# Chunked attention into a squared-ReLU FFN: V of odd heads in shifted tiles, all loads from SyncE, two groups transposed on TensorE

## The chip, the cores and the metric

The kernel runs on one core of a Trainium2 chip. A core has five engines with instruction streams of their own: TensorE (PE, matrix multiplication; PEld is its weight load), VectorE (DVE), ScalarE (ACT), GpSimd (POOL) and SyncE (SP), which only issues DMA transfers and waits. Each engine works through its own stream in program order and waits on semaphores. SP, ACT and POOL can issue DMAs; 16 DMA engines move the data. The metric is the device time of one execution in microseconds (us); lower is better. Where a profile is quoted, times count from the first instruction, and "span" is the time from the first to the last instruction.

## The reference

```python
# q, k, v: (8, 8, 576, 64) float32; chunk = 64
scores = scale * np.matmul(q_c, k_c.transpose(0, 1, 2, 4, 3))   # 64 x 64 per chunk and head
scores = scores - np.max(scores, axis=-1, keepdims=True)
attn = np.exp(scores)
attn = attn / (np.sum(attn, axis=-1, keepdims=True) + 1e-09)
out = np.matmul(attn, v_c)
x = out.transpose(0, 2, 1, 3).reshape(4608, 512)
h = np.maximum(x @ w_in, 0.0)          # w_in 512 x 2048
return (h * h @ w_out)                 # w_out 2048 x 512, result 4608 x 512 float32
```

Attention is block-diagonal: each chunk of 64 tokens attends to itself alone. Everything is float32 in memory.

## The kernel before, in words

The 4608 tokens form 18 groups of 256 (two tiles of 128, t = 0 and 1). Groups form nine blocks: block 0 is groups 0 to 2, blocks 1 to 7 are two groups each (3 and 4, 5 and 6, and so on), block 8 is group 17. A batch has 576 tokens, so some tiles cross from one batch to the next; `segments` and `runs` split such a load in two.

**Loads.** `qk_pieces(g)` loads q and k of a group with tokens on partitions, one DMA for each of q and k and each run of tokens: 256 KB for a whole tile, in pieces of 256 bytes (one head of one token). `v_pieces(g)` loads V into one of five `v_tiles` that have an extra column of ones per head, so that the values' matmul also gives the softmax's sum. Even heads go to the partition of their token (L100, 128 KB for a whole tile). For odd heads the two halves of a tile change places, so that the matmuls of an even and an odd head can work on different quarters of the array; each half is a DMA of its own (L104, 64 partitions, 64 KB). In the start-up and for groups 2 to 4 SP issues all of them; later the odd-head loads are issued by ACT. `load_w_in` and `load_w_out` load the weights in eight pieces each through five staging buffers; POOL casts each to bf16.

**Attention of a group** has four steps. (1) q and k are brought to head-dimension-on-partitions form in `qkT`. Groups 0 and 1 do it on PE through two FFN banks of PSUM (`transpose_qk_early`), group 2 on PE through an attention bank (`transpose_qk`, T), all others by a cast on POOL (`cast_qk`, C) and a DMA transpose that SP issues (`transpose_qk_dma`, TD, L202). (2) `scores` (SC, L216): 32 matmuls and one exponential on ACT. (3) `values` (AV, L235): matmuls with V, then reciprocal and multiplication on DVE, giving x. (4) x is transposed into `xT`: groups 0 and 1 on PE with copies by ACT (`transpose_x_early`), group 2 on PE with a copy by DVE, all others by DMA transposes from SP (`transpose_x`, XT, L258, two per group).

**FFN of a block.** `ffn_in` runs 16 column tiles of w_in; each is four matmuls (L288), a relu on ACT (L294) and a square on DVE (L295) into `gT`. `ffn_out` runs 16 matmuls per 128 tokens (L304), a copy by ACT (L311) and an output DMA issued by SP (L313).

**Order.** It is written out by hand. After the start-up (loads of groups 0 and 1, attention of both with idle PE time filled by `keep_busy`, then all weight loads and those of groups 2, 3 and 4), a block is a sequence of slots: one slot is four matmuls of the FFN. Block 0 has 56 slots (0 to 15 `ffn_in` for 512 tokens, 16 to 31 for the other 256, 32 to 55 `ffn_out`), a block of two groups has 32 (16 and 16). In each slot from `first_load` on, one more load of the block after next ("far") is issued, and then the attention steps that `plan` puts at this slot, for the next block ("nxt") or for far. Since every engine is in order, a step's place in the slots is its place in the streams of PE, SP, ACT, DVE and POOL alike.

Of the kernel before, what the change touches and what calls it, by code (L numbers as in the profile page):

```python
# [9 lines left out]
FP32 = mybir.dt.float32  # L10
BF16 = mybir.dt.bfloat16
# [5 lines left out]
def kernel(  # L17
# [9 lines left out]
    nc = tc.nc  # L27

    B, H, S, D = q.shape
    n_tokens = B * S  # L30
# [3 lines left out]
    n_hp = H // 2  # L34
# [9 lines left out]
    w_pool = ctx.enter_context(tc.tile_pool(name="w", bufs=1))  # L44
# [16 lines left out]


    NV = 5
    v_tiles = [w_pool.tile([128, 2, H, D + 1], FP32, name=f"v_sb{i}") for i in range(NV)]
    for vt in v_tiles:
        nc.gpsimd.memset(vt[:, :, :, D:D + 1], 1.0)

    def segments(g0, n):
        while n:
            b, s = divmod(g0, S)  # L70
            m = min(n, S - s)
            yield b, s, m
            g0 += m
            n -= m
# [3 lines left out]
    def runs(g):  # L78

        for t in range(GT // 128):  # L80
            p = 0
            for b, s, m in segments(g * GT + t * 128, 128):
                yield t, p, m, b, s
                p += m
# [8 lines left out]
                    out=dst[p:p + m, t, :, :],  # L93
                    in_=src[b, :, s:s + m, :].rearrange("h s d -> s h d"))

    def v_pieces(g, eng=(nc.sync, nc.sync)):

        vt = v_tiles[g % NV]
        for t, p, m, b, s in runs(g):
            yield lambda t=t, p=p, m=m, b=b, s=s: eng[0].dma_start(  # L100
                out=vt[p:p + m, t, 0::2, 0:D],
                in_=v[b, 0::2, s:s + m, :].rearrange("h s d -> s h d"))
            for c in range(0, m, 64):
                yield lambda t=t, p=64 - (p + c), b=b, s=s + c: eng[1].dma_start(  # L104
                    out=vt[p:p + 64, t, 1::2, 0:D],
                    in_=v[b, 1::2, s:s + 64, :].rearrange("h s d -> s h d"))

    def go(pieces):
        for f in pieces:
            f()  # L110

    def load_w_in(i, eng=nc.sync):
        cols = slice(i * 256, (i + 1) * 256)
        st = wst_pool.tile([128, 1024], FP32, name="w_st").rearrange("p (a f) -> p a f", a=n_dt)
        eng.dma_start(
            out=st, in_=moe_w_in[:, cols].rearrange("(a p) f -> p a f", p=128))
        nc.gpsimd.tensor_copy(out=w_in_bf[:, :, cols], in_=st)  # L117
# [37 lines left out]
    def transpose_qk_early(g, k_copy):  # L155
        qkT = att_pool.tile([128, 2, 2, n_hp, 128], BF16, name="qkT", bufs=4)
        state["qkT", g] = qkT
        banks = [ps_ffn.tile([128, 512], FP32, name="ps_ffn").bitcast(BF16) for _ in range(2)]
        for t in range(2):
            for which in range(2):  # L160
                srcb = qk[g][which].bitcast(BF16)
                for hp in range(n_hp):
                    c0 = t * 512 + hp * 128
                    nc.tensor.transpose(  # L164
                        out=banks[which][:, c0:c0 + 128],
                        in_=srcb[:, t, 2 * hp:2 * hp + 2, 1::2],
                        identity=ident)
        for which, copy in enumerate((nc.vector.tensor_copy, k_copy)):
            copy(out=qkT[:, which].rearrange("c t h q -> c (t h q)"), in_=banks[which])  # L169

    def transpose_x_early(g, t):
        j, c = place[g]
        if j not in xTs:
            xTs[j] = att_pool.tile([128, n_dt, BT], BF16, name="xT", bufs=2)
        psb = ps_ffn.tile([128, 512], FP32, name="ps_ffn").bitcast(BF16)
        x = state.pop(("x", g, t))
        for hp in range(n_hp):
            nc.tensor.transpose(  # L178
                out=psb[:, hp * 128:(hp + 1) * 128],
                in_=x[:, hp].rearrange("p a d -> p (a d)"),  # L180
                identity=ident)
        nc.scalar.copy(  # L182
            out=xTs[j][:, :, c + t * 128:c + (t + 1) * 128],
            in_=psb[:, 0:512].rearrange("p (h t) -> p h t", h=n_hp))

    def keep_busy(n):
        ps = ps_ffn.tile([128, 512], FP32, name="ps_ffn")
        for _ in range(n):
            nc.tensor.matmul(out=ps[:, 0:128], lhsT=ident, rhs=ident, start=True, stop=True)  # L189
# [35 lines left out]

    def values(g):
        e = state.pop(("e", g))
        vb = v_tiles[g % NV].bitcast(BF16)
        for t in range(2):
            ps = ps_att.tile([128, 2, 512], FP32, name="ps_att")  # L230
            for hp in range(n_hp):
                for a in range(2):
                    for p in range(2):
                        c = p ^ a
                        nc.tensor.matmul(  # L235
                            out=ps[64 * p:64 * p + 64, a, hp * (D + 1):(hp + 1) * (D + 1)],
                            lhsT=e[64 * c:64 * c + 64, a, hp, t, :],
                            rhs=vb[64 * c:64 * c + 64, t, 2 * hp + a, 1::2],
                            start=True, stop=True)
            o = ps[:, :, 0:n_hp * (D + 1)].rearrange("p a (h d) -> p a h d", d=D + 1)  # L240
            rec = att_pool.tile([128, 2, n_hp], FP32, name="rec", bufs=4)
            nc.vector.reciprocal(out=rec, in_=o[:, :, :, D])  # L242
            x = att_pool.tile([128, n_hp, 2, D], BF16, name="x", bufs=6)
            state["x", g, t] = x
            nc.vector.tensor_tensor(  # L245
                out=x.rearrange("p h a d -> p a h d"),
                in0=o[:, :, :, 0:D],
                in1=rec.to_broadcast([128, 2, n_hp, D]),
                op=ALU.mult)
# [25 lines left out]

    T, C, TD = transpose_qk, cast_qk, transpose_qk_dma
    SC, AV, XT = scores, values, transpose_x

    gTs = {}

    def ffn_in(j, c, n):
# [32 lines left out]
                if ft % 4 == 3:  # L314
                    yield

    def pieces(grps, eng=(nc.sync, nc.sync)):
        for g in grps:
            yield from qk_pieces(g)
        for g in grps:  # L320
            yield from v_pieces(g, eng)

    go(qk_pieces(0))
    go(qk_pieces(1))
    go(v_pieces(0))
    go(v_pieces(1))
    transpose_qk_early(0, nc.scalar.copy)
    keep_busy(8)
    SC(0)
    load_w_in(0, nc.scalar)  # L330
    keep_busy(8)
    transpose_qk_early(1, nc.vector.tensor_copy)
    keep_busy(8)
    SC(1)
    keep_busy(8)
    AV(0)
    keep_busy(6)
    AV(1)
    transpose_x_early(0, 0)
    transpose_x_early(0, 1)  # L340
    keep_busy(10)
    transpose_x_early(1, 0)
    transpose_x_early(1, 1)

    for i in range(1, 4):
        load_w_in(i)
    go(pieces([2]))
    for i in range(4, 8):
        load_w_in(i)
    for i in range(8):  # L350
        load_w_out(i)
    go(pieces(blocks[1]))

    for j, grps in enumerate(blocks):
        nxt = blocks[j + 1] if j + 1 < len(blocks) else []
        far = blocks[j + 2] if j + 2 < len(blocks) else []
        loads = pieces(far, (nc.sync, nc.scalar))
        plan = {}

        def at(slot, f, g):  # L360
            plan.setdefault(slot, []).append((f, g))

        if j == 0:
            first_load = 30
            for slot, f in ((7, T), (7, SC), (8, AV), (10, XT)):
                at(slot, f, 2)
            for i, g in enumerate(nxt):
                for slot, f in ((26, C), (30, TD), (43, SC), (46, AV), (47, XT)):
                    at(slot if f is SC else slot + 3 * i, f, g)
            for i, g in enumerate(far):  # L370
                at(46 + 2 * i, C, g)
                at(50 + 3 * i, TD, g)
            phases = [ffn_in(0, 0, 512), ffn_in(0, 512, 256), ffn_out(0)]
        else:
            first_load = 0
            for i, g in enumerate(nxt):
                for slot, f in ((1, SC), (5, AV), (8, XT)):
                    at(slot if f is SC else slot + 3 * i, f, g)
            for i, g in enumerate(far):
                at(14 + 2 * i, C, g)  # L380
                at(19 + 3 * i, TD, g)
            phases = [ffn_in(j, 0, len(grps) * GT), ffn_out(j)]
        slot = 0
        for phase in phases:
            for _ in phase:
                if slot >= first_load:
                    for f in loads:
                        f()
                        break
                for f, g in plan.get(slot, []):  # L390
                    f(g)
                slot += 1
        go(loads)
# [30 lines left out]
```

## Time and profile before

| | |
|---|---|
| median of 3 executions | 332.95 us (332.71 to 335.0) |
| the profiled execution's own time | 334.0 us |
| its span | 332.2 us |
| mean granted TensorE clock | 0.941 |
| PE busy | 289.4 us (87%) |
| ACT, DVE, POOL busy | 129.5, 110.1, 51.1 us |
| DMA | 58.35 MB in 172797 packets, 162016 of them under 512 B |
| chain that ended last | PE 70%, SP's queue 13%, DMA 10% |

The page gives busy time per engine, then the span in 40 slices with the busy share in tenths, the clock granted to PE and the DMA engines' share; then the chain of work that ended last, the costliest groups of instructions, and the DMA issues with the time to landing. A group's row ends with the idle time of its engine just before it and the work that ended this idle time. In a timeline the bracket at the end of a row says the same of a single stretch. A row with SPq or ACTq is an instruction of the queue of SyncE or ScalarE, mostly the issue of a DMA. DMA shares can exceed 1 where packets overlap.

### The profile page before, as it was taken

The page shows a single profiled execution, that of the slowest core. Times are in us where ns is not written, and L with a number is a line of the kernel's source. Part 1 is how long each engine was busy: PE and PEld are TensorE (multiplying, and loading weights), DVE is VectorE, ACT ScalarE, POOL GpSimd, SP SyncE. Part 2 cuts the span into 40 slices and gives each one's busy share as a digit, 9 for nine tenths or more (in the row PEclk, how much of TensorE's full clock was granted, in tenths as well). Part 3 has the DMA queues.
Part 4 walks back from the last instruction along what each step waited for, and adds up shares of the span by engine and source line. Part 5 has one row for each costly group of instructions (what it writes and reads, how often), then busy time and mean ns, then how long its engine had stood idle before and what let it go on. Part 6 is the DMA issues. An engine that isn't in the chain of part 4 may idle for free.

```text
span 332.2 us, 6218 instructions
## 1 busy us (share of the span) xinstructions
PE 289.4 (87%) x2488; PEld 142.4 (43%) x2488; DVE 110.1 (33%) x237; ACT 129.5 (39%) x221; POOL 51.1 (15%) x58
## 2 busy tenths in 40 slices
PE   2769699901964899999999999999999999999995
PEld 1653356401331444444444444444444444444572
DVE  0132398000221281067029206801820570162050
ACT  1324565101112452374265227415632751562261
POOL 1121276402200130022004101300220110000000
PEclk9956999975697799999999999999999999999999
DMA  9999899969968999799969999998999985110101
GB/s 172 227 235 158 271 386 270 193 134 214 231 139 183 213 180 172 179 214 171 201 175 193 197 213 206 194 201 205 164 172 218 236 90 126 65 32 33 65 33 63
DMA packets 172797, 58.35 MB, mean 176 GB/s; under 512 B 162016, under 2 KB 166112, under 8 KB 172768
## 3 DMA queue, kind: packets, MB, share of 16 engines
q1 hardware_dynamic: 158096, 54.02, 77.4%
q10 hardware_dynamic: 14672, 3.94, 8.1%
q8 instruction: 19, 0.31, 0.4%
q14 instruction: 10, 0.08, 0.1%
HBM read 36.70 MB, written 9.44 MB: 139 GB/s over the span
## 4 chain that ended last, share of the span: by engine, by line
PE 70%; SPq 13%; DMA 10%; DVE 3%; issue 1%; ACT 1%; ACTq 0%; POOL 0%
PE ps_ffn L304 34%; PE ps_ffn L288 32%; DMA v_sb<-in_v_dram 6%; SPq L92 5%; DMA qkT<-qkb 3%; SPq L104 3%; DVE gT L295 2%; SPq L100 2%; PE ps_att L235 2%; PE ps_att L216 1%; DMA w_st<-in_moe_w_in_dram 1%; SPq L258 1%; SPq L202 1%; ACT rl L294 1%; DVE x L245 1%
## 5 line engine op out<-in xcount | busy, mean ns | idle before, releaser
L288 PE MATMUL ps_ffn<-xT,w_in_bf 128*128 128x512 bf16 (+1 forms) x640 | 135.9, 368 | 7.2 <-DMA xT<-x 5.0
L295 DVE TENSOR_TENSOR gT<-rl 128x512 bf16<-128x512 bf16 (+1 forms) x160 | 78.4, 510 | 161.4 <-ACT rl L294 157.4
L304 PE MATMUL ps_ffn<-w_out_bf,gT 128*128 128x512 bf16 x576 | 129.2, 384 | 0.4 <-DVE gT L295 0.3
L294 ACT ACTIVATE rl<-ps_ffn 128x512 bf16<-128x512 f32 (+1 forms) x160 | 86.7, 556 | 59.7 <-PE ps_ffn L288 46.4
L288 PEld LDWEIGHTS <-w_in_bf 128*128 128x128 bf16 x640 | 62.0, 100 | 69.7 <-issue 14.1
L304 PEld LDWEIGHTS <-gT 128*128 128x128 bf16 x576 | 56.6, 99 | 69.5 <-issue 2.7
L311 ACT COPY o_sb<-ps_ffn 128x512 f32<-128x512 f32 x36 | 21.1, 586 | 101.7 <-PE ps_ffn L304 92.2
L195 POOL CAST qkb<-q_sb 128x1024 bf16<-128x1024 f32 x15 | 16.4, 1091 | 171.7 <-DMA q_sb<-in_q_dram 139.0
L223 ACT ACTIVATE e<-ps_att 128x1024 bf16<-128x1024 f32 x18 | 17.9, 1023 | 22.5 <-PE ps_att L216 19.2
L216 PE MATMUL ps_att<-qkT 64*64 64x64 bf16 x576 | 7.9, 205 | 21.0 <-DMA qkT<-qkb 18.6
L245 DVE TENSOR_TENSOR x<-ps_att,rec 128x512 bf16<-128x512 f32 x36 | 24.9, 691 | 1.2
L242 DVE RECIPROCAL rec<-ps_att 128x8 f32<-128x8 f32 x36 | 7.2, 200 | 37.8 <-PE ps_att L235 37.8
L195 POOL CAST qkb<-k_sb 128x1024 bf16<-128x1024 f32 x15 | 16.6, 1105 | 7.0 <-DMA k_sb<-in_k_dram 6.8
L216 PEld LDWEIGHTS <-qkT 64*64 64x64 bf16 x576 | 6.4, 117 | 25.7 <-DMA qkT<-qkb 20.1
L117 POOL CAST w_in_bf<-w_st 128x1024 bf16<-128x1024 f32 x8 | 8.6, 1074 | 33.7 <-DMA w_st<-in_moe_w_in_dram 33.7
L235 PE MATMUL ps_att<-v_sb,e 64*64 64x65 bf16 x576 | 10.1, 200 | 3.8 <-DMA v_sb<-in_v_dram 3.3
L235 PEld LDWEIGHTS <-e 64*64 64x64 bf16 x576 | 7.2, 110 | 12.2 <-issue 5.2
L124 POOL CAST w_out_bf<-w_st 128x1024 bf16<-128x1024 f32 x8 | 8.8, 1097 | 3.0 <-DMA w_st<-in_moe_w_out_dram 3.0
L164 PE MATMUL ps_ffn<-ident,q_sb 128*128 128x128 bf16 x16 | 2.5, 310 | 4.9 <-DMA q_sb<-in_q_dram 4.9
L169 DVE COPY qkT<-ps_ffn 128x1024 bf16<-128x1024 bf16 x3 | 2.1, 691 | 12.0 <-PE ps_ffn L164 12.0
L189 PE MATMUL ps_ffn<-ident 128*128 128x128 bf16 x48 | 5.5, 285 | 0.0
L182 ACT COPY xT<-ps_ffn 128x512 bf16<-128x512 bf16 x4 | 2.1, 589 | 7.6 <-PE ps_ffn L178 7.6
(25 smaller groups left out, 23.5 us busy)
## 6 DMA issues: line engine op xcount, KB each, us to landing
out_dram<-o_sb SPq DMA_DIRECT2D x36, 256.0 KB, 2.5
q_sb<-in_q_dram SPq DMA_DIRECT2D x32, 256.0 KB, 4.7
k_sb<-in_k_dram SPq DMA_DIRECT2D x32, 256.0 KB, 5.3
v_sb<-in_v_dram SPq DMA_DIRECT2D x32, 128.0 KB, 4.1
w_st<-in_moe_w_out_dram SPq DMA_DIRECT2D x8, 512.0 KB, 6.6
w_st<-in_moe_w_in_dram SPq DMA_DIRECT2D x7, 512.0 KB, 5.2
v_sb<-in_v_dram ACTq DMA_DIRECT2D x52, 64.0 KB, 3.8
v_sb<-in_v_dram SPq DMA_DIRECT2D x28, 64.0 KB, 3.2
```

The source lines that it names most:

```text
L92: yield lambda e=e, dst=dst, src=src, b=b, s=s, t=t, p=p, m=m: e.dma_start(out=dst[p:p + m, t, :, :], in_=src[b, :, s:s + m, :].rearrange( ...
L104: yield lambda t=t, p=64 - (p + c), b=b, s=s + c: eng[1].dma_start(out=vt[p:p + 64, t, 1::2, 0:D], in_=v[b, 1::2, s:s + 64, :].rearrange(" ...
L195: nc.gpsimd.tensor_copy(out=qkb[:, which], in_=qk[g][which].rearrange("p t h d -> p (t h d)"))
L216: nc.tensor.matmul(out=ps[64 * c:64 * c + 64, o0:o0 + 64], lhsT=qkT[64 * a:64 * a + 64, 1, t, hp, cols], rhs=qkT[64 * a:64 * a + 64, 0, t, ...
L223: nc.scalar.activation(out=e.rearrange("p a h t q -> p (a h t q)"), in_=ps, func=AF.Exp, scale=scale)
L235: nc.tensor.matmul(out=ps[64 * p:64 * p + 64, a, hp * (D + 1):(hp + 1) * (D + 1)], lhsT=e[64 * c:64 * c + 64, a, hp, t, :], rhs=vb[64 * c: ...
L245: nc.vector.tensor_tensor(out=x.rearrange("p h a d -> p a h d"), in0=o[:, :, :, 0:D], in1=rec.to_broadcast([128, 2, n_hp, D]), op=ALU.mult)
L288: nc.tensor.matmul(out=h[:, 0:n], lhsT=w_in_bf[:, dt, ft * 128:(ft + 1) * 128], rhs=xT[:, dt, c:c + n], start=(dt == 0), stop=(dt == n_dt ...
L294: nc.scalar.activation(out=rl[:, 0:n], in_=h[:, 0:n], func=AF.Relu)
L295: nc.vector.tensor_tensor(out=gT[:, ft, c:c + n], in0=rl[:, 0:n], in1=rl[:, 0:n], op=ALU.mult)
L304: nc.tensor.matmul(out=o_ps, lhsT=gT[:, ft, tt * 128:(tt + 1) * 128], rhs=w_out_bf[:, ft, :], start=(ft == 0), stop=(ft == n_ft - 1))
L311: nc.scalar.copy(out=o_sb, in_=o_ps)
```

## The change

Six things change together.

1. V has two sets of tiles. `v_even` (five) hold even heads with each token on its own partition. `v_odd` (eleven) hold odd heads in tiles that start 64 tokens ahead: odd tile n covers tokens 128n - 64 to 128n + 63, so that the second half of one token tile lies on partitions 0 to 63 and the first half of the next on 64 to 127. An odd tile is one DMA of 128 partitions (128 KB), but for the first and the last, which are half, and for three that cross into another batch and take two. `v_pieces(g)` loads odd tiles 2g + 1 and 2g + 2, and also 0 for group 0. V takes 80 DMAs in all, before 120.
2. All loads of the groups are issued by SP; ACT issues none of V. The two sets need 16 memsets of their columns of ones in place of 5.
3. Groups 3 and 4 are transposed on PE (`transpose_qk`, slots 40 and 42 of block 0); their casts (slots 26 and 29) and DMA transposes (30 and 33) are gone.
4. Group 2 uses the early forms: q and k by `transpose_qk_early` at slot 7, x by `transpose_x_early` at slot 10. Its scores move from slot 7 to slot 8, where its values are too.
5. Other slots: in block 0 the far loads start at slot 32, not 30; scores of groups 3 and 4 at 44, not 43; values at 47 and 50, not 46 and 49; x transposes at 49 and 52, not 47 and 50; casts of groups 5 and 6 at 47 and 50, their DMA transposes at 53 and 55, before 46, 48, 50 and 53. In the other blocks scores, values and x transposes of the next block are three slots later (4, 8 and 11 in place of 1, 5 and 8); casts and DMA transposes of the far block stay.
6. The start-up has 68 `keep_busy` matmuls in place of 48, in other places.

```diff
-    v_tiles = [w_pool.tile([128, 2, H, D + 1], FP32, name=f"v_sb{i}") for i in range(NV)]
+    NO = 2 * NV + 1
+    v_even = [w_pool.tile([128, 2, n_hp, D + 1], FP32, name=f"ve_sb{i}") for i in range(NV)]
+    v_odd = [w_pool.tile([128, n_hp, D + 1], FP32, name=f"vo_sb{i}") for i in range(NO)]
...
-    def v_pieces(g, eng=(nc.sync, nc.sync)):
-        vt = v_tiles[g % NV]
+    def v_pieces(g):
         for t, p, m, b, s in runs(g):
-            yield lambda t=t, p=p, m=m, b=b, s=s: eng[0].dma_start(
-                out=vt[p:p + m, t, 0::2, 0:D],
+            yield lambda t=t, p=p, m=m, b=b, s=s: nc.sync.dma_start(
+                out=v_even[g % NV][p:p + m, t, :, 0:D],
                 in_=v[b, 0::2, s:s + m, :].rearrange("h s d -> s h d"))
-            for c in range(0, m, 64):
-                yield lambda t=t, p=64 - (p + c), b=b, s=s + c: eng[1].dma_start(
-                    out=vt[p:p + 64, t, 1::2, 0:D],
-                    in_=v[b, 1::2, s:s + 64, :].rearrange("h s d -> s h d"))
+        for n in ([0] if g == 0 else []) + [2 * g + 1, 2 * g + 2]:
+            lo, hi = max(0, 128 * n - 64), min(n_tokens, 128 * n + 64)
+            p = lo - (128 * n - 64)
+            for b, s, m in segments(lo, hi - lo):
+                yield lambda n=n, p=p, m=m, b=b, s=s: nc.sync.dma_start(
+                    out=v_odd[n % NO][p:p + m, :, 0:D],
+                    in_=v[b, 1::2, s:s + m, :].rearrange("h s d -> s h d"))
+                p += m
...
-        vb = v_tiles[g % NV].bitcast(BF16)
+        veb = v_even[g % NV].bitcast(BF16)
+        vob = [v_odd[(2 * g + n) % NO].bitcast(BF16) for n in range(3)]
...
+                        vb = vob[t + p] if a else veb[:, t]
...
-                            rhs=vb[64 * c:64 * c + 64, t, 2 * hp + a, 1::2],
+                            rhs=vb[64 * c:64 * c + 64, hp, 1::2],
...
+    def TE(g):
+        transpose_qk_early(g, nc.scalar.copy)
+
+    def XE(g):
+        for t in range(2):
+            transpose_x_early(g, t)
...
     transpose_qk_early(0, nc.scalar.copy)
-    keep_busy(8)
+    keep_busy(10)
     SC(0)
     load_w_in(0, nc.scalar)
+    keep_busy(10)
+    transpose_qk_early(1, nc.vector.tensor_copy)
+    keep_busy(12)
+    SC(1)
+    keep_busy(10)
+    AV(0)
+    keep_busy(10)
+    AV(1)
+    XE(0)
     keep_busy(8)
-    transpose_qk_early(1, nc.vector.tensor_copy)
+    XE(1)
     keep_busy(8)
...
-        loads = pieces(far, (nc.sync, nc.scalar))
+        loads = pieces(far)
...
-            first_load = 30
-            for slot, f in ((7, T), (7, SC), (8, AV), (10, XT)):
+            first_load = 32
+            for slot, f in ((7, TE), (8, SC), (8, AV), (10, XE)):
                 at(slot, f, 2)
             for i, g in enumerate(nxt):
-                for slot, f in ((26, C), (30, TD), (43, SC), (46, AV), (47, XT)):
-                    at(slot if f is SC else slot + 3 * i, f, g)
+                for slot, f in ((40 + 2 * i, T), (44, SC), (47 + 3 * i, AV), (49 + 3 * i, XT)):
+                    at(slot, f, g)
             for i, g in enumerate(far):
-                at(46 + 2 * i, C, g)
-                at(50 + 3 * i, TD, g)
+                at(47 + 3 * i, C, g)
+                at(53 + 2 * i, TD, g)
...
-                for slot, f in ((1, SC), (5, AV), (8, XT)):
+                for slot, f in ((4, SC), (8, AV), (11, XT)):
```

More of the change, by code (lines that the diff above doesn't have):

```diff
@@ L63 @@
     NV = 5
-    v_tiles = [w_pool.tile([128, 2, H, D + 1], FP32, name=f"v_sb{i}") for i in range(NV)]
-    for vt in v_tiles:
+    NO = 2 * NV + 1
+    v_even = [w_pool.tile([128, 2, n_hp, D + 1], FP32, name=f"ve_sb{i}") for i in range(NV)]
+    v_odd = [w_pool.tile([128, n_hp, D + 1], FP32, name=f"vo_sb{i}") for i in range(NO)]
+    for vt in v_even:
         nc.gpsimd.memset(vt[:, :, :, D:D + 1], 1.0)
+    for vt in v_odd:
+        nc.gpsimd.memset(vt[:, :, D:D + 1], 1.0)
     def segments(g0, n):
@@ L315, in ffn_out, with pieces @@
                     yield
-    def pieces(grps, eng=(nc.sync, nc.sync)):
+    def pieces(grps):
         for g in grps:
@@ L320, in pieces @@
         for g in grps:
-            yield from v_pieces(g, eng)
+            yield from v_pieces(g)
     go(qk_pieces(0))
@@ L327 @@
     transpose_qk_early(0, nc.scalar.copy)
-    keep_busy(8)
+    keep_busy(10)
     SC(0)
     load_w_in(0, nc.scalar)
+    keep_busy(10)
[7 more added lines that the diff above has]
+    XE(0)
     keep_busy(8)
-    transpose_qk_early(1, nc.vector.tensor_copy)
+    XE(1)
     keep_busy(8)
[L334 to L343, printed above, removed]
     for i in range(1, 4):
```

## The prediction

> **What bounds the kernel now.** I read the page's slices first, then a table by stages, then TensorE's (PE) and SyncE's (SP) lines in order of time. Slices are 8.3 us wide, digits are busy tenths:
>
> ```profile
> PE   2769699901964899999999999999999999999995
> ...
> DMA  9999899969968999799969999998999985110101
> ```
>
> From the fourteenth slice on PE is full: the second half can only be pushed by PE work itself. The holes lie before it, while the DMA engines are loaded throughout. The windows are cut at the stages: a PE hole, the rest of block 0's second matmul, a hole, block 1, block 2, block 3.
>
> ```profile
> 66.20:82.40 16.20, 0.66 (x36) 0.52 (x36) 0.00 (x0) 1.61 (x2) 2.03 (x2) 0.66 0.82 170
> 82.40:97.10 14.70, 14.69 (x144) 6.25 (x144) 3.41 (x8) 2.20 (x3) 2.03 (x2) 0.80 0.87 203
> 97.10:102.10 5.00, 0.00 (x0) 0.02 (x1) 0.00 (x0) 0.59 (x1) 0.00 (x0) 1.00 0.45 94
> 102.10:138.50 36.40, 33.00 (x257) 14.63 (x258) 10.87 (x24) 13.15 (x21) 4.25 (x4) 0.91 1.01 197
> 138.50:168.60 30.10, 29.69 (x258) 13.48 (x256) 12.29 (x24) 13.34 (x22) 4.51 (x4) 1.00 1.03 193
> 168.60:198.00 29.40, 29.40 (x258) 13.58 (x256) 11.92 (x24) 13.34 (x22) 4.70 (x4) 1.00 1.08 192
> ```
>
> The last three figures of a row are granted clock, DMA share and GB/s. A clean block takes 29.4 us; block 1 takes 36.4. A granted clock of 0.80 over 14.7 us is 2.9 us lost, 0.91 over 36.4 is 3.3. The bracket in PE's timeline names who ended each hole:
>
> ```profile
> 76.39 0.64 PE L216 MATMUL ps_att<-qkT 64*64 64x64 bf16 x32 [10.22 <-DMA qkT<-qkb]
> 82.39 0.64 PE L216 MATMUL ps_att<-qkT 64*64 64x64 bf16 x32 [5.35 <-DMA qkT<-qkb]
> ...
> 102.11 3.53 PE L288 MATMUL ps_ffn<-xT,w_in_bf 128*128 128x512 bf16 x8 [5.02 <-DMA xT<-x]
> ...
> 109.04 0.64 PE L216 MATMUL ps_att<-qkT 64*64 64x64 bf16 x32 [3.02 <-DMA qkT<-qkb]
> ```
>
> So PE waits 15.6 us for the DMA transposes of groups 3 and 4, 5.0 for x of block 1, 3.0 for group 6. Why so late? SP issues in program order:
>
> ```profile
> 60.40 1.47 SPq L100 DMA_DIRECT2D v_sb<-in_v_dram  x1
> ...
> 69.67 1.27 SPq L104 DMA_DIRECT2D v_sb<-in_v_dram  x2
> ...
> 71.68 3.09 SPq L202 DMA_TRANSPOSE qkT<-qkb  x1
> ...
> 77.32 3.29 SPq L202 DMA_TRANSPOSE qkT<-qkb  x1
> ...
> 94.83 2.54 SPq L258 DMA_TRANSPOSE xT<-x  x2
> ```
>
> The first two rows are the ends of V of groups 3 and 4: twelve issues from 60.40 to 70.94, and only then comes group 3's transpose. The DMA engines were not the limit there (window columns: length, clock, DMA share, GB/s):
>
> ```profile
> 18.00:20.00 2.00, 0.50 0.51 103
> ...
> 66.00:72.00 6.00, 0.94 0.45 103
> ```
>
> They are half idle: the issuing is the limit. Its prices are the issue times by line (min/median/max ns):
>
> ```profile
> L92 SPq DMA_DIRECT2D q_sb<-in_q_dram x40: 427/936/3220, 0.7 to 259.0; - x40
> L100 SPq DMA_DIRECT2D v_sb<-in_v_dram x40: 374/604/2241, 8.6 to 263.4; - x40
> L104 ACTq DMA_DIRECT2D v_sb<-in_v_dram x52: 602/616/1495, 62.8 to 267.2; - x52
> L202 SPq DMA_TRANSPOSE qkT<-qkb x15: 1357/3055/3434, 71.7 to 276.8; - x15
> L258 SPq DMA_TRANSPOSE xT<-x x30: 1190/1230/2513, 94.8 to 295.1; - x30
> L313 SPq DMA_DIRECT2D out_dram<-o_sb x36: 332/359/1236, 81.3 to 329.2; - x36
> ```
>
> A 64-partition odd load takes as long to issue as a 128-partition even one.
>
> **The change part by part.** *Fewer V issues.* Groups 0 and 1 go from 12 to 9, group 2 from 7 to 5, groups 3 and 4 from 12 to 9. The early ones lead to PE's weight wait:
>
> ```profile
> 8.65 1.10 SPq L100 DMA_DIRECT2D v_sb<-in_v_dram  x1
> ...
> 15.90 2.35 SPq L104 DMA_DIRECT2D v_sb<-in_v_dram  x2
> ...
> 28.30 1.63 SPq L100 DMA_DIRECT2D v_sb<-in_v_dram  x1
> ...
> 32.61 1.26 SPq L104 DMA_DIRECT2D v_sb<-in_v_dram  x2
> ```
>
> ```profile
> 37.98 1.04 POOL L117 CAST w_in_bf<-w_st 128x1024 bf16<-128x1024 f32 x1 [9.43 <-DMA w_st<-in_moe_w_in_dram]
> ```
>
> ```profile
> 39.08 1.04 PE L288 MATMUL ps_ffn<-xT,w_in_bf 128*128 128x512 bf16 x4 [0.95 <-POOL w_in_bf L117]
> ```
>
> The first twelve fill 8.65 to 18.25; nine at 0.604 with some 0.05 between, the first at 1.10, end near 15.0, 3.2 earlier; group 2 saves two, 1.3. The new 128-partition odd load is not in the trace; its nearest row is L100, between 0.374 and the 1.63 above, and I take its median. Of the 4.5 I count 3.4 (bounds 0 and 4.5), since in other stretches the engines were full. All later SP work moves with it. Groups 3 and 4 take 9 x 0.65 = 5.8 in place of 10.5: 4.7 more. SP ends their V at 70.9 - 3.4 - 4.7 = 62.8.
>
> *Group 2 by the early form.* Scores and values now share slot 8, so PE's values, and all of PE behind them, wait for one exponential.
>
> ```profile
> 38.19 1.02 ACT L223 ACTIVATE e<-ps_att 128x1024 bf16<-128x1024 f32 x1 [0.56 <-PE ps_att L216]
> ...
> 34.73 0.61 PE L143 MATMUL ps_att<-ident,q_sb 128*128 128x128 bf16 x8
> 35.17 0.61 PE L143 MATMUL ps_att<-ident,k_sb 128*128 128x128 bf16 x8
> ```
>
> That is 1.0 plus the relu ahead of it: I put 1.7 (bounds 0 and 2), so PE gains 3.4 - 1.7 = 1.7 at the start of block 0's second matmul.
>
> *Warm-up and memsets.* Twenty more warm-up matmuls and eleven more memsets:
>
> ```profile
> L189 PE MATMUL ps_ffn<-ident 128*128 128x128 bf16 x48 | 5.5, 285 | 0.0
> ```
>
> ```profile
> 1.59 0.31 POOL L66 MEMSET v_sb<- 128x16 f32 x5
> 15.44 1.04 POOL L117 CAST w_in_bf<-w_st 128x1024 bf16<-128x1024 f32 x1 [13.53 <-DMA w_st<-in_moe_w_in_dram]
> ```
>
> Twenty at 5.5/48 are 2.3 us inside PE's waits for loads; uncovered they cost that, and a warmer clock may give a microsecond back. Memsets hide in POOL's 13.5. Both zero.
>
> *Groups 3 and 4 on PE.* The 15.6 us go, and the 2.9 us of low clock behind them. Added: two rounds of 16 transposes, 0.44 per 8, 1.75 together. New wait: T(3) and T(4) stand in PE's order at slots 40 and 42 and hold up everything behind them if q and k are late. In the trace POOL casts the last of them at
>
> ```profile
> 64.67 1.04 POOL L195 CAST qkb<-k_sb 128x1024 bf16<-128x1024 f32 x1
> ```
>
> so they land near 61.3 after the shift, and T(4) comes near 64.2: cover 2.9; without the shift it waits 0.5. The copies go to idle VectorE and to ScalarE. PE ends block 0 at 97.1 - 15.6 - 2.9 + 1.75 - 1.7 = 78.6.
>
> *What is late next: x of block 1.* XT(4) is in SP's order behind everything of slots 32 to 52. From 62.8: ten q/k at 0.936 (9.4), nine V at 0.604 (5.4), five outputs at 0.359 (1.8), four x transposes at 1.23 (4.9), 28 gaps of 0.05 (1.4): 22.9, so the last issue ends at 85.7. Its landing comes from the chain:
>
> ```profile
> 99.50 2.47 DMA xT<-x
> ```
>
> 85.7 - 1.23 + 2.47 = 86.9. PE waits 8.3 us there, up from 5.0, and block 1 starts at 86.9, not 102.1. With each issue at its minimum (0.427, 0.374, 0.332, 1.19) it is 15.5 and 79.6; with no V saving, 95.0.
>
> *Block 1.* Its scores move from slot 1 to 4. Group 6's transpose follows XT(4) by two of 3.1 and one output, so it lands near 93; slot 4 comes some 6 us after the start, at 93: the 3.0 goes. The clock will be low again after 8.3 us of idleness: between the 1.7 (half of 3.3) that the 5.0 us hole cost and the 2.9 of the 16 us one, I take 2.4. Block 1: 29.4 + 2.4 = 31.8, ending at 118.7 instead of 138.5.
>
> By the Trainium skill, "TensorE: Matmul & The Clock Gate", Part 1, the clock halves after an idle window of about 3.4 us and needs about 3.4 us of work to return: that would be 1.7 here, sum 0.7 lower.
>
> *Later blocks.* ScalarE loses 52 issues (32 us); PE hardly waited for it, and block 2's 0.7 over 29.4 is all I give. SP takes over half of them, 20 more in all.
>
> **The sum.** 332.2 - 19.8 - 0.7 = 311.7 of span; with the 1.8 around it 313.5 against this execution's 334.0. The median shown is 1.05 below that: 312.4.
>
> **Rivals.** *Merged loads save nothing*, since bytes and packets stay: start at 95.0, 8.1 later, 320.5. For: DMA share near 1.0 in most slices. Against: 103 GB/s while SP issued V back to back. The Trainium skill, "DMA: Bandwidth & Descriptors", Issuing engines are not separate DMA queues, speaks for it: which engine issues saves only sequencer time, usually small. Here the 0.45 share shows it is not small.
>
> *SP issues at its minima*: start at 79.6, 1.0 after PE is ready, no cold clock: 29.5 + 0.7 off, 302.7. Against: medians are twice that whenever queues are full.
>
> *SP becomes the bound, and the kernel slower.* In the five blocks that load two groups SP now issues 9 q/k (8.4), 9 V (5.4), 4 x (4.9), 2 transposes (6.1), 4 outputs (1.4), gaps (1.4): 27.6 of 29.4. It decides from 29.4 on, when V costs over 0.8 each. At 1.37, the mean of the 1.10 and 1.63 above, it is 34.5, 5.1 per block: 25.5 more, 337.9. Against: SP waits for outputs with time to spare,
>
> ```profile
> SPq L313 <- ACT o_sb L311: 55.8, 21, 10.0
> ```
>
> *The hole only moves*: x lands at 102 as before, from slow q/k issues; block 1 saves its 3.0 and no more, about 329.
>
> **How the numbers follow.** Forecast 0.66, own range 307 to 317; merged loads save nothing 0.13; SP at its minima 0.08; SP the bound 0.09, of which a third ends slower and the rest between 317 and 329; the hole moves 0.04. From 305 to 321 all but about 0.18 is held. One per cent, 3.3 us, is about what can be told from no change: faster 0.94, same 0.03, slower 0.03.
>
> **What would show it.** No wait for qkT before block 0's scores; the largest PE hole a wait for xT near 79 to 87; V loads at 0.6 each with 128 partitions; first w_in cast of the second half near 34.6; blocks from 2 on at 29.4. I am wrong if PE waits for q_sb or k_sb at the new transposes, if later blocks lengthen, or if the wait for xT exceeds 13.

## The result and the profile after

The changed kernel takes 318.79 us (median, 318.31 to 319.72) against 333.82 us of the kernel before in the same comparison: a ratio of 0.9553, 95% interval 0.9505 to 0.96. The forecast was 312.4 us, with a range of 305 to 321 over all rivals: the sign and this range hold, but the middle was 6.4 us too low, and the time lies above the 307 to 317 that the forecast gave for itself. The profiled execution took 319.72 us with a span of 317.9, against 334.0 and 332.2.

On PE's timeline after, two holes of over 1.2 us are left behind the first FFN matmul, those of the first and the third row; the second row is the start of block 0's second matmul (the bracket is the idle time before the row and who ended it):

```profile
37.37 1.46 PE L304 MATMUL ps_ffn<-xT,w_in_bf 128*128 128x512 bf16 x3 [5.19 <-POOL w_in_bf L124]
...
57.12 7.93 PE L320 MATMUL ps_ffn<-w_out_bf,gT 128*128 128x512 bf16 x35
...
90.87 7.12 PE L304 MATMUL ps_ffn<-xT,w_in_bf 128*128 128x512 bf16 x20 [9.34 <-DMA xT<-x]
```

No wait for qkT is left: the 15.6 us before block 0's scores and the 3.0 us in block 1 are gone. The wait for xT has grown from 5.0 to 9.3 us, close to the forecast's 8.3, but it ends at 90.87, not at 86.9. The first row is a wait that had been 0.95 and that I had expected to shrink.

The windows after, cut at the stages (length, PE, PEld, DVE, ACT, POOL, granted clock, DMA share, GB/s): the hole, the slow start of block 1, its rest, then blocks 2 to 6.

```profile
81.50:90.90 9.40, 0.06 (x2) 0.13 (x2) 0.00 (x0) 0.58 (x1) 0.11 (x1) 0.74 0.68 175
90.90:96.20 5.30, 5.30 (x13) 1.90 (x13) 0.85 (x2) 1.21 (x3) 0.00 (x0) 0.50 1.10 260
96.20:123.10 26.90, 26.69 (x241) 12.37 (x244) 10.60 (x22) 11.64 (x19) 4.48 (x4) 1.00 0.92 203
123.10:152.60 29.50, 29.29 (x254) 13.72 (x257) 10.93 (x24) 13.44 (x22) 4.67 (x4) 1.00 0.94 197
152.60:182.60 30.00, 29.35 (x254) 13.64 (x256) 11.72 (x24) 13.44 (x22) 4.75 (x4) 1.00 0.91 193
182.60:212.20 29.60, 29.33 (x254) 13.61 (x257) 11.51 (x24) 13.44 (x22) 4.40 (x4) 1.00 0.95 196
212.20:241.80 29.60, 29.35 (x254) 13.65 (x257) 10.91 (x24) 13.44 (x22) 4.43 (x4) 1.00 0.94 166
241.80:271.80 30.00, 29.34 (x254) 13.65 (x257) 10.98 (x24) 13.44 (x22) 2.41 (x2) 1.00 0.66 152
```

Block 1 takes 32.2 us (36.4 before), and 5.3 us of it run at half clock. Later blocks take 29.5 to 30.0, where a clean one had 29.4.

SP's rows after, from V of groups 3 and 4 to the last x transpose of block 1:

```profile
58.23 3.11 SPq L103 DMA_DIRECT2D ve_sb<-in_v_dram  x2
...
63.58 1.91 SPq L110 DMA_DIRECT2D vo_sb<-in_v_dram  x3
...
87.17 2.53 SPq L267 DMA_TRANSPOSE xT<-x  x2
```

V ends at 65.5 instead of 70.9, and the last x transpose is issued to 89.7 and lands as block 1 starts. Between two of SP's issues in this stretch lie 0.5 us at most.

### The profile page after: what moved, and what is told of

Read it like the earlier page. It is cut to its first block, busy times and chain, and to the rows that moved or that the text cites. A ratio compares the mean times of both kernels' runs of the same rounds, so it can differ in the third digit from the quotient of the medians.

```text
span 317.9 us, 6266 instructions
## 1 busy us (share of the span) xinstructions
PE 285.3 (90%) x2504; PEld 144.3 (45%) x2540; DVE 108.0 (34%) x238; ACT 132.0 (42%) x225; POOL 47.6 (15%) x65
## 4 chain that ended last, share of the span: by engine, by line
PE 80%; SPq 6%; DVE 3%; issue 3%; DMA 3%; ACT 2%; another core or an unknown queue 2%; ACTq 0%
PE ps_ffn L320 39%; PE ps_ffn L304 36%; SPq L96 2%; PE ps_att L244 2%; DVE gT L311 2%; DMA vo_sb<-in_v_dram 2%; ACT rl L310 2%; SPq L267 1%; SPq L103 1%; PE ps_att L223 1%; SPq L110 1%; DMA xT<-x 1%; PE ps_ffn L185 1%; PE ps_att L150 1%
## 5 line engine op out<-in xcount | busy, mean ns | idle before, releaser
L304 PE MATMUL ps_ffn<-xT,w_in_bf 128*128 128x512 bf16 (+1 forms) x617 | 133.7, 367 | 16.1 <-DMA xT<-x 9.3
L311 DVE TENSOR_TENSOR gT<-rl 128x512 bf16<-128x512 bf16 (+1 forms) x160 | 75.5, 493 | 166.0 <-ACT rl L310 162.2
L320 PE MATMUL ps_ffn<-w_out_bf,gT 128*128 128x512 bf16 x563 | 125.6, 379 | 0.8 <-issue 0.2
L310 ACT ACTIVATE rl<-ps_ffn 128x512 bf16<-128x512 f32 (+1 forms) x160 | 86.9, 557 | 61.9 <-PE ps_ffn L304 48.1
L202 POOL CAST qkb<-q_sb 128x1024 bf16<-128x1024 f32 x13 | 14.7, 1129 | 163.7 <-DMA q_sb<-in_q_dram 163.7
L202 POOL CAST qkb<-k_sb 128x1024 bf16<-128x1024 f32 x13 | 14.9, 1145 | 5.0 <-DMA k_sb<-in_k_dram 4.9
L244 PE MATMUL ps_att<-ve_sb,e 64*64 64x65 bf16 x288 | 10.3, 202 | 3.2 <-ACT e L230 1.1
L244 PE MATMUL ps_att<-vo_sb,e 64*64 64x65 bf16 x288 | 10.4, 202 | 1.9 <-DMA vo_sb<-in_v_dram 1.9
L223 PE MATMUL ps_att<-qkT 64*64 64x64 bf16 x576 | 7.2, 199 | 0.5 <-issue 0.4
L196 PE MATMUL ps_ffn<-ident 128*128 128x128 bf16 x68 | 6.8, 267 | 0.0
L176 DVE COPY qkT<-ps_ffn 128x1024 bf16<-128x1024 bf16 x4 | 2.8, 690 | 11.6 <-PE ps_ffn L171 11.6
```

The costliest lines, as they stand in the source:

```text
L202: nc.gpsimd.tensor_copy(out=qkb[:, which], in_=qk[g][which].rearrange("p t h d -> p (t h d)"))
L223: nc.tensor.matmul(out=ps[64 * c:64 * c + 64, o0:o0 + 64], lhsT=qkT[64 * a:64 * a + 64, 1, t, hp, cols], rhs=qkT[64 * a:64 * a + 64, 0, t, ...
L244: nc.tensor.matmul(out=ps[64 * p:64 * p + 64, a, hp * (D + 1):(hp + 1) * (D + 1)], lhsT=e[64 * c:64 * c + 64, a, hp, t, :], rhs=vb[64 * c: ...
L304: nc.tensor.matmul(out=h[:, 0:n], lhsT=w_in_bf[:, dt, ft * 128:(ft + 1) * 128], rhs=xT[:, dt, c:c + n], start=(dt == 0), stop=(dt == n_dt ...
L310: nc.scalar.activation(out=rl[:, 0:n], in_=h[:, 0:n], func=AF.Relu)
L311: nc.vector.tensor_tensor(out=gT[:, ft, c:c + n], in0=rl[:, 0:n], in1=rl[:, 0:n], op=ALU.mult)
```

## The experiments

Times are medians, ratios are to the kernel before measured beside them; "block 1" is its first matmul in one profile. To judge such single times I ran the changed kernel a second time:

> The changed kernel again, unaltered, as the measure of scatter beside the next two. Expected 318 to 320; in its profile block 1 starts between 89 and 92, blocks 2 to 6 take 29.4 to 30.1 each, and PE's wait for xT is 8 to 10 us. If the start of block 1 moves by more than 2 us between its two profiles, differences of that size between single profiles mean nothing.

It took 319.58 us (317.69 to 321.58), ratio 0.9553 (0.9511 to 0.9596), as the first time, but in its profile block 1 started at 88.8 instead of 90.87, and the span was 315.9. A difference of 2 us between two profiles in the start of block 1 therefore says nothing; the ratios, and waits that come or go, do.

**Groups 3 and 4 transposed by DMA again.**

```diff
-                for slot, f in ((40 + 2 * i, T), (44, SC), (47 + 3 * i, AV), (49 + 3 * i, XT)):
+                for slot, f in ((26 + 3 * i, C), (30 + 3 * i, TD), (44, SC), (47 + 3 * i, AV), (49 + 3 * i, XT)):
```

> The changed kernel, but groups 3 and 4 are cast on POOL (slots 26, 29) and transposed by DMA (slots 30, 33) as before; all else stays changed. Theory (the 15.6 us hole was SP reaching these transposes late, and TensorE removes it): SP ends V of group 4 at 65.5, so the two transposes are issued to about 72 and land near 75; PE stands at the scores of slot 44 from about 68 to 75 (a wait for qkT of 6 to 9 us), and all later SP work moves back by 6.4, so XT(4) lands near 97 and block 1 starts there, not at 90.9. Time about 325 (span 324). Rival (SP's order past the V loads is all that matters, and x of block 1 is as late either way): PE waits at the scores instead of at xT, block 1 starts at 91 to 92, time 319 to 320.

321.36 us, ratio 0.9649 (0.9604 to 0.9695): only about 1% of the kernel before is lost. That lies between the theory (325) and the rival (319 to 320), nearer to the rival. The holes on PE in this kernel:

```profile
68.69 0.45 PE L223 MATMUL ps_att<-qkT 64*64 64x64 bf16 x32 [1.12 <-DMA qkT<-qkb]
73.54 0.64 PE L223 MATMUL ps_att<-qkT 64*64 64x64 bf16 x32 [4.41 <-DMA qkT<-qkb]
...
94.28 4.02 PE L304 MATMUL ps_ffn<-xT,w_in_bf 128*128 128x512 bf16 x9 [7.57 <-DMA xT<-x]
```

With the DMA transposes back, 5.5 of the 15.6 us come back, not all. Block 1 starts 3.4 us later, at 94.3, not 97. SP reaches the transposes early because V is out of the way:

```profile
64.51 2.18 SPq L209 DMA_TRANSPOSE qkT<-qkb  x1
...
68.56 2.75 SPq L209 DMA_TRANSPOSE qkT<-qkb  x1
```

That is 7.2 and 8.8 us before the 71.68 and 77.32 of the kernel before.

**V alone, all else as before.** The new tiles, their loads and the two lines in `values`, put into the kernel before; all loads from SP.

> The kernel before with nothing but the new V tiles and their loads, all issued by SP; start-up, transposes and slots stay as before. Theory (the hole of 15.6 us before block 0's scores was made mostly by the V issues in front of the DMA transposes): SP ends V of groups 3 and 4 some 5 us earlier, near 65.5, the waits for qkT shrink from 15.6 to 8 to 10, block 1 starts at 95 to 97 instead of 102, time 324 to 327 (6 to 9 of the 14 us). Rival (the transposes on TensorE make the gain, V only helps them): the waits stay at 13 or more, time 329 or more.

322.03 us, ratio 0.9649 (0.9603 to 0.9695), better than expected.

```profile
69.49 0.64 PE L223 MATMUL ps_att<-qkT 64*64 64x64 bf16 x32 [5.13 <-DMA qkT<-qkb]
75.09 0.64 PE L223 MATMUL ps_att<-qkT 64*64 64x64 bf16 x32 [4.95 <-DMA qkT<-qkb]
93.57 3.60 PE L297 MATMUL ps_ffn<-xT,w_in_bf 128*128 128x512 bf16 x8 [5.26 <-DMA xT<-x]
99.23 0.64 PE L223 MATMUL ps_att<-qkT 64*64 64x64 bf16 x32 [1.49 <-DMA qkT<-qkb]
```

The V part by itself brings 3.5% where the whole change brings 4.5%: the two waits fall from 15.6 to 10.1, block 1 starts at 93.6 instead of 102.1.

**All but V.** The mirror: the changed kernel with the old V tiles, odd halves from SP at first and from ACT later.

> The changed kernel, but V in the tiles of before: odd heads in half-tile loads of 64 partitions, issued by SP for groups 0 to 4 and by ACT for later ones. Theory (fewer issues bring SP forward): V of group 4 ends on SP near 70.9 instead of 65.5, 5.4 later; four to five odd loads of groups 5 and 6 leave SP again, 2.3 earlier, so XT(4) lands some 3 later, at 94, and the time is 321 to 323. Rival (merging saves nothing since the bytes stay): 318 to 319. Rival (taking the issues from ACT is what counts): ACT's copies and relus wait behind V issues and blocks 2 to 6 become longer than 29.7.

325.92 us (324.66 to 329.65), ratio 0.9786 (0.9723 to 0.9849); more than the 321 to 323 of the theory, though block 1 starts at 93.9, where the theory had it. There is no wait for qkT before block 0's scores, and the wait for xT is 12.5 us:

```profile
57.94 2.41 SPq L100 DMA_DIRECT2D v_sb<-in_v_dram  x1
...
66.80 1.26 SPq L104 DMA_DIRECT2D v_sb<-in_v_dram  x2
...
90.10 2.56 SPq L258 DMA_TRANSPOSE xT<-x  x2
```

```profile
93.94 7.13 PE L295 MATMUL ps_ffn<-xT,w_in_bf 128*128 128x512 bf16 x20 [12.49 <-DMA xT<-x]
```

V of groups 3 and 4 takes SP 10.1 us here (57.94 to 68.06) and 7.3 in the changed kernel (58.23 to 65.49), with the same bytes. It ends 2.6 later, and the last x transpose is issued 3.0 later (92.66 and 89.70). So merging saves issue time: the rival by which it saves nothing falls. Without the V part the change is worth 2.3% less by the two ratios. Not all of this is merging: blocks 2 to 6, with ACT issuing odd halves, take 149.6 us here and 148.7 and 148.5 in the two profiles of the changed kernel, about 1 us, which is what the last rival names.

The two halves alone give 3.5% and 2.1%, together 4.5%. They do not add; my explanation, argued and not tried, is that both shorten the same queue and that PE had been waiting at two places of it. Two counts belong here. The kernel before issues V in 112 DMAs (40 at L100, 72 at L104), not 120. And group 2's early forms and the start-up's warm-up, which are in this kernel and not in the one before it, were never tried alone.

**Odd tiles of the later groups issued by ACT.**

```diff
-        loads = pieces(far)
+        loads = pieces(far, nc.scalar)
```

The new argument is the engine that issues the odd tiles; `pieces` hands it on to `v_pieces` (lines left out here).

> The changed kernel, but the whole odd tiles of groups 5 and later are issued by ACT, not SP. Theory (SP has room in the later blocks, but not before block 1): four issues of 0.55 leave SP ahead of XT(4), so block 1 starts about 2 earlier, at 88.5 to 89; blocks 2 to 6 keep their 29.6 to 30.0; time 316 to 317.5. Rival (SP is the bound in the later blocks too): they come down to 29.4, time 314 to 315. Rival (ACT's time is what the change freed): ACT gets behind, time 320 or more.

320.54 us, ratio 0.9622 (0.9581 to 0.9663): the interval overlaps that of the changed kernel's 0.9553, and block 1 starts at 90.2, inside the scatter. The four issues fewer on SP did not show, and the trace has a reason: SP stood still elsewhere. From the end of V of group 4 to that of the last x transpose it takes 25.5 us here and 24.2 in the changed kernel, and in between it waits 6.3 us, in three pieces, for V loads:

```profile
66.12 0.70 SPq L329 DMA_DIRECT2D out_dram<-o_sb  x1
71.14 0.37 SPq L96 DMA_DIRECT2D k_sb<-in_k_dram  x1
```

```profile
SPq L96 <- DMA vo_sb<-in_v_dram: 6.3, 3, 4.3
```

Each of the three ends as a V load that ACT issued lands. The kernel with all but V has such waits too (6.4 us in two pieces), and in the kernel before the first x transpose was held 1.9 us by one; the changed kernel has none. Why a load of q or k waits for them was not tried. So "SyncE alone issues loads" is worth nothing in time that could be measured, but as the balance of two effects: more issues on SP, and no waits for loads of the other queue. With the odd tiles of groups 5 and later issued by ACT the merged loads keep most of the gain, 3.8% of 4.5% by the ratios.

The Trainium skill, "DMA: Bandwidth & Descriptors", Issuing engines are not separate DMA queues, says that issuing from several engines saves only sequencer time, usually small beside the DMA itself. The ratios agree that the choice of engine gains nothing. For one V load the time is small too (a median of 0.54 to 0.58 us of issue, 3.0 to 3.2 to landing), but in an in-order queue it adds up: nine issues in place of twelve are 7.3 us in place of 10.5.

**PE kept busy while it waits for w_in.** `keep_busy(56)` behind the transposes of group 2.

> The changed kernel with 56 more warm-up matmuls behind the transposes of group 2 (slot 7), where PE waits 5.2 us for the cast of w_in and the granted clock then falls to 0.74 to 0.75 until 50 us. Theory (SP's order sets the start of block 1, PE's own lateness there is hidden): the clock stays at 1.0, block 0's second matmul starts near 54.5 to 55 instead of 57.1, PE ends block 0 some 2 us earlier, the wait for xT grows from 9.3 to 11 or more, and the time stays within 318 to 319.5. Rival (the PE chain before block 1 is on the path): the time falls by the 2 us, to 316.5.

316.93 us, ratio 0.9515 (0.9484 to 0.9547): the interval overlaps that of the changed kernel, though the four executions (316.47 to 317.29) all lie below the ten of the changed kernel (317.69 to 321.58). Neither expectation holds whole. Block 0's second matmul still starts at 56.9, so what sets it is not PE's clock at 37 us; block 1 starts at 90.4, as the theory had it; and the time is near the rival's. In the profile the difference lies behind that: block 1 takes 30.7 us, against 32.2 and 32.4 in the two profiles of the changed kernel, mostly because the clock stays at 0.50 for only 2.7 us of it and not for 5.2 or 5.3. Blocks 2 to 6 take 147.4 against 148.7 and 148.5, but 147.7 in the kernel of the first experiment, whose slots there are the same. Whether the warm-up shortens the slow start of block 1, 50 us later, or the one profile did so by chance, is open.

**x of groups 3 and 4 on PE.** One constant, `FIRST_DMA_X = 5`.

> The changed kernel, but x of groups 3 and 4 is transposed on PE too (copies by VectorE), so the four DMA transposes that SP issued last before block 1 are gone. Theory (block 1 waits for SP's order, 9.3 us): the wait for xT goes, block 1 starts at 82 to 84; but SP brings the transposes of groups 5 and 6 only 4.9 earlier, so PE now waits 4 to 6 us for qkT of group 6 at slot 4 of block 1. Time 314 to 316. Rival (DMA throughput, not SP's order, is the limit): group 6's transpose lands no earlier than the 97.8 of the changed kernel, PE waits 10 us there, time 318 to 320.

314.35 us, ratio 0.9423 (0.938 to 0.9465), as the theory had it, with 3.1 us of new wait where it had 4 to 6. The wait for xT is gone, and what was next in SP's order is what PE waits for:

```profile
82.05 4.48 PE L304 MATMUL ps_ffn<-xT,w_in_bf 128*128 128x512 bf16 x20
87.40 0.45 PE L223 MATMUL ps_att<-qkT 64*64 64x64 bf16 x32 [0.86 <-DMA qkT<-qkb]
90.09 0.64 PE L223 MATMUL ps_att<-qkT 64*64 64x64 bf16 x32 [2.25 <-DMA qkT<-qkb]
```

**q and k of groups 5 and 6 on PE as well.**

```diff
-                at(47 + 3 * i, C, g)
-                at(53 + 2 * i, TD, g)
+                at(53 + 2 * i, T, g)
```

> As the last, and q and k of groups 5 and 6 are transposed on PE as well (slots 53 and 55 of block 0), without casts and DMA transposes. Theory: no wait of over 2 us between 45 us and the end; block 1 starts at 84 to 86 with a full clock and lasts 29.5 to 30; time 309 to 312. Rival (loads of groups 5 and 6 are late as well, DMA throughput): PE waits for q_sb or k_sb of group 6 before block 1, or for V in it, by 4 us or more; time 315 or more.

308.81 us, ratio 0.9247 (0.9213 to 0.928). No hole of over 1.2 us is left behind 45 us; block 1 starts at 83.8 and runs as a clean one:

```profile
83.80:113.00 29.20, 28.99 (x252) 13.53 (x256) 10.75 (x25) 13.56 (x22) 4.16 (x4) 1.00 0.96 209
```

The loads of groups 5 and 6 were in time, so the rival by which they are late falls; what had held block 1 was the place of the transposes in SP's order.

**Old slots from block 2 on.**

```diff
-                for slot, f in ((4, SC), (8, AV), (11, XT)):
+                for slot, f in (((4, SC), (8, AV), (11, XT)) if j == 1 else ((1, SC), (5, AV), (8, XT))):
```

> The changed kernel, but from block 2 on the scores, values and x transposes of the next block are at slots 1, 5 and 8 as before (block 1 keeps 4, 8 and 11). Theory (at slot 4 ScalarE's two exponentials make the squares late just when POOL's casts begin, and PE loses 0.2 to 0.6 us in some blocks): blocks 2 to 6 come down from 29.4 to 30.0 to 29.4, time 1 to 2 us shorter, 317 to 318. Rival (SP alone issues the loads, so the transposes for the next block are later): PE waits for qkT at slot 1 in some blocks, time 319 or more. Rival (scatter of single executions): no difference.

316.69 us, ratio 0.9484 (0.9455 to 0.9514); the interval just touches that of the changed kernel, so the blocks decide. Blocks 2 to 6, all five:

```profile
121.40:150.80 29.40, 29.19 (x254) 13.56 (x257) 11.65 (x24) 13.33 (x22) 4.31 (x4) 1.00 0.97 197
150.80:180.20 29.40, 29.19 (x254) 13.62 (x257) 11.91 (x24) 13.22 (x22) 4.16 (x4) 1.00 0.86 169
180.20:209.50 29.30, 29.09 (x254) 13.51 (x257) 11.60 (x24) 13.44 (x22) 4.37 (x4) 1.00 0.97 203
209.50:238.90 29.40, 29.19 (x254) 13.61 (x257) 11.90 (x24) 13.22 (x22) 4.58 (x4) 1.00 1.02 196
238.90:268.30 29.40, 29.19 (x254) 13.61 (x257) 10.29 (x24) 13.44 (x22) 2.08 (x2) 1.00 0.70 151
```

146.9 us in place of 148.7 for the windows above, without one wait for qkT: the transposes are early enough with V on SP alone. The other profiles bear it out: with the late slots these five blocks take 147.4 to 148.8 us in every kernel that has V on SP, with slots 1, 5 and 8 they take 146.8 (V alone, this one, and the one with both together below). The three slots cost 0.1 to 0.4 us per block. PE loses it at the values, where it waits for the multiplication on VectorE that gives x; in block 3 after:

```profile
164.97 0.22 PE L244 MATMUL ps_att<-ve_sb,e 64*64 64x65 bf16 x2 [0.44 <-DVE x L254]
```

The squares on VectorE ahead of it, behind the two exponentials, and POOL's casts beside them:

```profile
159.97 3.26 DVE L311 TENSOR_TENSOR gT<-rl 128x512 bf16<-128x512 bf16 x4 [1.90 <-ACT rl L310]
```

```profile
160.51 1.27 POOL L202 CAST qkb<-q_sb 128x1024 bf16<-128x1024 f32 x1 [22.31 <-DMA q_sb<-in_q_dram]
161.73 1.23 POOL L202 CAST qkb<-k_sb 128x1024 bf16<-128x1024 f32 x1
```

and the same squares with the scores at slot 1, before the casts begin:

```profile
155.61 1.44 DVE L311 TENSOR_TENSOR gT<-rl 128x512 bf16<-128x512 bf16 x3 [1.90 <-ACT rl L310]
```

0.82 us each beside a cast, 0.48 without. That the slots cost the time is shown; that the casts slow the squares is read from their coincidence, not tried by itself. With the old slots squares still fall beside casts later in the block and are as slow (0.91 us each from 159.51), and PE loses nothing: the cost comes where they stand behind the exponentials as well.

**Both together, and w_in earlier.** The last two put the findings into one kernel: x of 3 and 4 and q, k of 5 and 6 on PE, all later blocks at slots 1, 5 and 8; then also two pieces of w_in ahead of V of group 2.

> x of groups 3 and 4 and q, k of groups 5 and 6 on PE, and scores, values and x transposes of all blocks after the first at slots 1, 5 and 8 as before the change. Theory (the three slots cost 0.2 to 0.6 us in some blocks, and with group 6 transposed on PE nothing in block 1 needs them): blocks from 2 on at 29.4, 306.5 to 308. Rival (V of groups 5 and 6 or a transpose for a later block is now late): a PE wait of over 1 us in block 1 or 2, 309 or more.

308.39 us, ratio 0.9209 (0.9177 to 0.924): blocks from 2 on take 29.4 each; the time is 0.4 above what the theory gave, but without the waits that the rival named.

```diff
-    go(pieces([2]))
-    for i in range(4, 8):
+    go(qk_pieces(2))
+    for i in range(4, 6):
+        load_w_in(i)
+    go(v_pieces(2))
+    for i in range(6, 8):
         load_w_in(i)
```

> As the last, and the fifth and sixth piece of w_in are loaded ahead of V of group 2. Theory (PE's 4.8 us wait for the fifth piece in the start-up is SP's order: five V issues and their bytes stand ahead of it, and now PE's lateness there is no longer hidden by the wait for xT): the wait falls to 2 to 3, block 0's second matmul starts 1 to 2 earlier, time 1 to 2 us shorter than the last. Rival (the end of block 0's first part is set by w_out's bytes and the squares on VectorE): second matmul within 0.5 of the last, same time. Rival (V of group 2 is now late for its values): PE waits there instead, same time or longer.

306.19 us, ratio 0.9139 (0.9099 to 0.9178). The rows of the last kernel, then of the one without the reordering:

```profile
34.22 1.04 PE L304 MATMUL ps_ffn<-xT,w_in_bf 128*128 128x512 bf16 x4 [1.62 <-POOL w_in_bf L124]
...
52.13 4.06 PE L320 MATMUL ps_ffn<-w_out_bf,gT 128*128 128x512 bf16 x18 [0.21 <-ACT rl L310]
```

```profile
36.79 1.89 PE L304 MATMUL ps_ffn<-xT,w_in_bf 128*128 128x512 bf16 x4 [5.29 <-POOL w_in_bf L124]
...
57.02 1.24 PE L320 MATMUL ps_ffn<-w_out_bf,gT 128*128 128x512 bf16 x5
```

The wait falls by 3.7, and block 0's second matmul starts 4.9 us earlier, more than expected. Of this 2.2 us arrive in the time: PE now comes to the scores of block 2's slot 1 before a DMA transpose has landed, and waits 1.3 us there. In the changed kernel the wait for xT of 9.3 us stands behind this place, and the gain would, I expect, be lost in it; that was not run.

## Why the prediction was right, and where it was off

*The mechanism held.* SP's issue order set the start of block 1: block 1 comes forward when issues leave the queue in front of it (V alone; x transposes gone), goes back when they return (all but V; DMA transposes of groups 3 and 4 back), and stays when only PE is changed. Merging V did this with the same bytes. The next wait was named, xT. That its size came out close (8.3, measured 9.34) is partly luck: PE ended block 0 at 81.5, not 78.6, and x landed at 90.9, not 86.9, so both ends of the wait were late.

*The clock.* The cold start of block 1 cost 2.65 us (5.3 at half clock), forecast 2.4. The size is not fixed: in the other six profiles with a wait for xT of 7.6 to 12.5 us before block 1, the clock stays at 0.50 for 2.7 to 5.4 us, read in slices of 0.5 us. The rule quoted from the Trainium skill, "TensorE: Matmul & The Clock Gate", Part 1, about 3.4 us of work until the clock is back, would have given 1.7. Six of the seven profiles are above that and one (2.7 us, in the kernel with 56 more warm-up matmuls) is below, so neither one number from the rule nor one from a single profile serves here.

*The step on groups 3 and 4 gave the credit to the wrong part.* It let TensorE remove the whole 15.6 us. The runs show that the V part had made a third of that hole (10.1 left with V alone) and that with V merged and the other slots changed 5.5 remain for TensorE to remove, worth about 1% in time. The sum did not suffer, since the start of block 1 was worked out from SP's queue and not from PE's waits.

*The sum.* The forecast span was 311.7, the measured one 317.9. Of the 6.2 us, 4.0 are the later start of block 1, 0.4 its length and 1.8 the later blocks. Three terms were mis-sized:

- "SP ends their V at 62.8": 65.5. The shift of 3.4 did arrive at the first load of group 3 (46.29 instead of 49.64), and was given back inside the stretch: q and k of both groups took 11.9 us (10.7 before), V 7.3 where I had 5.8. The new odd load has a median of 0.54 us over the run, below the 0.60 of the forecast, but these nine V issues took 0.81 each, with a DMA share of 0.97 from 56 to 66 us. From there to the last x transpose SP took 24.2, not 22.9. Block 1 is 4.0 us late by these two.
- "PE gains 1.7 at the start of block 0's second matmul": it lost 1.5 (57.12 instead of 55.65). PE ran its first 32 matmuls faster (7.4 against 9.5 us), and then waited 5.19 for w_in, whose cast came 1.7 earlier, not 3.4. The kernel with V alone, which has neither the early forms of group 2 nor the longer warm-up, starts there at 53.84. So V does bring 1.8 us, and the rest of the start-up takes 3.3 back in this profile and 1.4 in the second one (55.27); which part of it does was not tried. It cost nothing in this kernel, because the wait for xT follows; the last experiment shows what time at this place is worth once that wait is gone.
- "Block 2's 0.7 is all I give" for the later blocks: they lost 1.8 against that. I had asked only whether SP could feed the moved slots, not what the moved slots collide with. Of the signs of being wrong that the prediction lists, this one came in part: blocks 2 to 6 take 148.7 us, 147.6 before.

One reading of the prediction was too wide as well. That the DMA engines are half idle while SP issues V rested on 66 to 72 us; in the kernel before, too, the first half of this V had run at a share of 0.88 (columns: length, clock, share, GB/s):

```profile
60.00:66.00 6.00, 1.00 0.88 187
```

*The rivals.* Merged loads save nothing: refuted, with the same bytes SP's issue time for V falls from 10.1 to 7.3 us and the ratio differs by 2.3%. SP issues at its minima: refuted, the stretch that would take 15.5 us took 24.2. SP the bound in later blocks: refuted; they are 29.4 as soon as the slots are back, with SP still issuing everything. The hole only moves: it did move, but x landed 11 us earlier than before, not at the same time.

## What to carry to other kernels

Where an in-order queue issues everything, count issues ahead of the item that the bottleneck waits for, and price the whole queue up to it: two edits that shorten the same queue need not add, and the engine that gets the credit in the wait list may not be the one that made the wait. When a wait goes, name the next item in the same queue and look at whether it can leave it too; here that was worth another 1.3% and then 1.8% of the time. A step moved to give one engine slack needs its neighbours at the new place checked as well. And when an experiment shows no difference, look in its trace for two effects that cancel.

## What the hardware showed that I had not expected

After a run of large weight pieces one or two of the q and k loads take several times their median to issue, and in this profile the DMA engines then fall to less than half their share. In the changed kernel:

```profile
46.81 2.62 SPq L96 DMA_DIRECT2D k_sb<-in_k_dram  x1
49.47 3.43 SPq L96 DMA_DIRECT2D q_sb<-in_q_dram  x1
```

```profile
28.00:30.00 2.00, 2.00 (x11) 0.88 (x9) 1.00 (x3) 1.47 (x3) 0.00 (x0) 1.00 0.43 94
52.00:54.00 2.00, 1.92 (x18) 1.58 (x17) 1.89 (x4) 1.41 (x5) 1.65 (x2) 1.00 0.42 83
```

2.6 and 3.4 us against a median of 0.9, then 83 GB/s for 2 us, although SP goes on issuing; at 28 us, behind w_in, it is alike, after k loads of 2.4 and 2.7 us. The long issue recurs, the fall in share less so: the second profile of the changed kernel has a q load of 3.44 us, and then a share of 0.91 with 173 GB/s at 50 to 52. The kernel before has one such issue, 3.22 us at 51.31. What holds it back was not tried; in the changed kernel it is part of the 2.7 us by which V ended later than forecast.
